# A memory-augmented transformer on one core: the recorded order of its tasks from the 1200th on replaced by another

## The chip, the cores and the metric

The kernel runs on one core of one Trainium2 chip. Its time is the device time of one execution in microseconds (us); the profile of that execution starts with the first instruction and ends with the last. The engines are PE (TensorE, the matmuls), PEld (the weight loads of PE, which overlap its matmuls), DVE (VectorE), ACT (ScalarE), POOL (GpSimd) and SP (SyncE). SP and POOL also issue the transfers (DMA): SP on the queue called hardware_dynamic, POOL on the one called software_dynamic.

## The reference

Two pairs of layers on x of 2048 x 512 in bf16: an attention with a recurrent memory, a gated feed-forward network, and both once more with the same weights.

```python
def _A_ref(x, mem0, Wq, Wk, Wv, Wo, seg_len):      # 32 heads of 128, 8 memory rows, segments of 32
    mem = mem0
    for s in range(n_seg):                          # 64 segments, one after another
        h = jnp.concatenate([mem, x[:, s * seg_len:(s + 1) * seg_len, :]], axis=1)
        q, k, v = (jnp.einsum('btd,dhe->bhte', h, W) for W in (Wq, Wk, Wv))
        scores = jnp.where(mask, jnp.einsum('bhqe,bhke->bhqk', q, k) * scale, -1000000000.0)
        o = jnp.einsum('bhqk,bhke->bhqe', _softmax(scores), v)
        o = jnp.einsum('bhte,hed->btd', o, Wo)
        mem = o[:, :M, :]                           # the memory of the next segment
        outs.append(o[:, M:, :])

def _B_ref(x, w_gate, w_up, w_down):                # 512 -> 1792 -> 512
    return jnp.einsum('bsf,fd->bsd', _sigmoid(x @ w_gate) * (x @ w_up), w_down)

x = x + _A_ref(_layernorm(x), ...)
x = x + _B_ref(_layernorm(x), ...)
x = x + _A_ref(_layernorm(x), ...)
x = x + _B_ref(_layernorm(x), ...)
```

(Shortened: the reference writes the three projections and the products out one by one.)

## The kernel before

**Steps.** The segments of one attention layer depend on each other through the memory, so the kernel goes through them in 70 steps (`emit_step(t)`). From step 6 on the second attention layer runs six segments behind the first, and one step does segment t of layer 1 and segment t - 6 of layer 2 together, with 2 x 40 = 80 columns. Four segments make a block; after each block a feed-forward pass (`ffn`) follows for its 128 rows, with the weights streamed again each time.

**One step.** PE makes q and k for three heads at a time (line 868, weights wq_sb and wk_sb stay in SBUF), ACT copies them out of the bank (qku), PE makes the scores (line 904), DVE and ACT do the softmax (lines 918 to 939), PE transposes the probabilities (line 950), ACT or DVE copies them (ptsb), PE multiplies them with the values (line 976), ACT copies that (otsb), and PE multiplies with wo_sb (line 995). The values are not where line 976 needs them: the part that depends on the memory is made in `strips` (line 762), copied to sst, and moved by transfers into vsb (`add_strips`); the part that depends on x alone is made ahead for a block (`v_pass`, line 635), copied to vst, written to the DRAM scratch scr, and read back into vsb. Line 976 waits for all of these transfers (the keys "vs" and "vx"). The feed-forward pass multiplies with wg and wu (line 1097) and wd (line 1120), which POOL loads in pieces of 256 KB (lines 1089, 1090 and 1114).

**What sets the order.** `trace` first adds 13,976 tasks to a `Planner`, each with the engines that may run it, a planned duration, and the keys that it reads and writes. A task on PE is a group of matmuls. `Planner.plan` doesn't search: it reads the order of all tasks, and one bit for each task that may run on either of two engines (copies: ACT or DVE; many transfers: SP or POOL), from SEQUENCE, a packed text in the file. The order gives each engine its own in-order program and also decides which buffers and banks a task gets.

**What the planner derives from the order.** `replay` goes through the tasks in the recorded order with a model of durations and transfer latencies (the constants LAT, BUS, LEAD, TAIL and others) and gives each task a planned start. Two things are made from these. For a weight load on POOL of 300,000 modelled bytes or more it picks a PE task (`pace`), and `run` makes the load wait for that task. And `warm` looks at the planned idle time of PE ahead of each PE task:

```python
            if gap > 250.0 and on:                              # line 346
                ...
                if cold or lo < 0.6 * self.SPAN:
                    n = int((gap - 120.0) * 2.4 - (min(tk.start, self.COLD) - end) * 1.2 * cold) // P
                    if n > 0:
                        fill[tk.idx] = (on[0], n)
```

Here `on` are the banks that the task takes, `lo` is the least planned PE work in a stretch of SPAN = 3413 ns around the gap, `cold` is true only near the start, and n counts groups of 128 columns. `run` then issues, ahead of such a task, matmuls of zeros (the tile hot) into that bank, of up to 512 columns each, on line 1214. They are called fillers below. `replay` and `warm` are the same code in both kernels.

Of the kernel before, what the change touches and what calls it, by code (L numbers as in the profile page):

```python
# [1293 lines left out]
```

## Time and profile before

| | us |
|---|---|
| median of 3 runs | 1747.95 |
| lowest and highest of them | 1744.44 and 1748.0 |
| span of the profiled execution | 1747.1 |
| PE busy | 1733.4 |
| DVE busy | 1248.4 |
| ACT busy | 1128.5 |
| POOL busy | 859.0 |

The span runs from the first to the last instruction of the execution that was profiled; no other time of that execution is shown. Lines such as "L868 PE MATMUL bank<-hT,wq_sb 128x80 x6656 | 485.9, 202 | 0.0" are groups: line of the kernel, engine, operation, output and inputs, shape, count, then busy time, mean duration of one in ns, and idle time of the engine before them. In a timeline the first number is the start, the second the length of the merged piece; the pieces overlap, since a matmul's record includes its way through the array, so that the distance between starts is what a matmul costs PE. A wait line names who waited, for what, the total, the number of times and the longest.

### The profile page before, as it was taken

The numbers are of one execution on the slowest core, as the hardware profiler recorded it, in microseconds if no ns is written. First come the engines' busy times: TensorE is split into PE (matmuls) and PEld (weight loads), VectorE is DVE, ScalarE is ACT, GpSimd is POOL, SyncE is SP. The second block draws the span as 40 slices with busy tenths as digits, with TensorE's granted clock in tenths as the row PEclk, the third lists the DMA queues.
The fourth block names the chain that finished last, engine by engine and source line by source line (L and its number), as shares of the span: only waits on it lengthen the run. The fifth ranks groups of instructions, "written<-read, shape, count | busy, mean of one in ns | idle before, by whom it ended". The sixth has DMA issues, their size and how long they took to land.

```text
span 1747.1 us, 91842 instructions
## 1 busy us (share of the span) xinstructions
PE 1733.4 (99%) x39162; PEld 1491.8 (85%) x39162; DVE 1248.4 (71%) x4208; ACT 1128.5 (65%) x3119; POOL 859.0 (49%) x1367
## 2 busy tenths in 40 slices
PE   9999999999999999999999999999999999999998
PEld 4688789889898988989888888989888888988886
DVE  5677777677767776786777767776777776767676
ACT  3576777566666766666666666666665666666564
POOL 5624345635544554445445554544455364454543
PEclk9999999999999999999999999999999999999999
DMA  8935355645645555545555464545455464554644
GB/s 285 320 100 155 109 151 161 195 113 153 174 130 163 156 159 143 165 125 164 152 148 158 136 184 128 166 138 153 132 174 166 139 174 128 144 156 131 178 120 134
DMA packets 145583, 273.41 MB, mean 156 GB/s; under 512 B 39686, under 2 KB 86018, under 8 KB 145174
## 3 DMA queue, kind: packets, MB, share of 16 engines
q0 software_dynamic: 72944, 198.79, 39.8%
q1 hardware_dynamic: 72230, 68.75, 13.3%
q8 instruction: 307, 5.03, 1.2%
q14 instruction: 102, 0.84, 0.2%
HBM read 221.78 MB, written 27.07 MB: 142 GB/s over the span
## 4 chain that ended last, share of the span: by engine, by line
PE 94%; DMA 3%; DVE 1%; SPq 1%; issue 1%; POOL 0%; ACT 0%; POOLq 0%; ACTq 0%
PE bank L868 34%; PE bank L995 17%; PE bank L1097 12%; PE bank L762 8%; PE bank L635 6%; PE bank L1120 6%; PE bank L904 4%; PE bank L976 4%; PE bank L950 2%; PE bank L595 1%; PE bank L1214 1%; DMA wk_sb<-in_A_Wk_dram 1%; DMA wo_sb<-in_A_Wo_dram 0%; PE bank L1065 0%; DMA scr<-wu 0%
## 5 line engine op out<-in xcount | busy, mean ns | idle before, releaser
L868 PE MATMUL bank<-hT,wq_sb 128*128 128x80 bf16 (+3 forms) x8960 | 616.4, 198 | 1.0 <-DVE hT L1008 0.3
L868 PE MATMUL bank<-hT,wk_sb 128*128 128x80 bf16 (+3 forms) x8960 | 616.3, 198 | 0.8 <-DMA wk_sb<-in_A_Wk_dram 0.6
L1228 ACT CAST qku<-bank 128x480 bf16<-128x480 f32 (+4 forms) x770 | 384.7, 508 | 223.7 <-PE bank L868 194.6
L868 PEld LDWEIGHTS <-wq_sb 128*128 128x128 bf16 x8960 | 454.2, 99 | 32.1 <-issue 15.1
L868 PEld LDWEIGHTS <-wk_sb 128*128 128x128 bf16 x8960 | 446.9, 99 | 1.1 <-DMA wk_sb<-in_A_Wk_dram 0.7
L995 PE MATMUL bank<-otsb,wo_sb 128*128 128x80 bf16 (+1 forms) x8960 | 360.2, 198 | 2.2 <-DMA wo_sb<-in_A_Wo_dram 1.3
L918 DVE TENSOR_TENSOR st<-bank,cst 40x240 f32<-40x240 f32 (+3 forms) x768 | 280.5, 368 | 113.2 <-PE bank L904 97.5
L995 PEld LDWEIGHTS <-wo_sb 128*128 128x128 bf16 x8960 | 336.6, 99 | 15.5 <-DMA wo_sb<-in_A_Wo_dram 2.0
L1228 ACT CAST otsb<-bank 128x480 bf16<-128x480 f32 (+3 forms) x420 | 200.2, 483 | 83.4 <-PE bank L976 52.8
L1090 POOL DMA_DIRECT2D wu<-in_B_w_up_dram x217 | 166.5, 768 | 170.0 <-PE bank L950 36.4
L1114 POOL DMA_DIRECT2D wd<-in_B_w_down_dram x217 | 156.9, 723 | 182.0 <-PE bank L1120 39.6
L1224 POOL DMA_DIRECT2D vsb<-sst x351 | 178.2, 512 | 129.6 <-ACT sst L1228 64.7
L1089 POOL DMA_DIRECT2D wg<-in_B_w_gate_dram x217 | 166.4, 767 | 138.1 <-PE bank L1097 56.7
L928 ACT ACTIVATE st<-st 80x240 f32<-80x240 f32 (+3 forms) x420 | 159.2, 381 | 58.0 <-DVE st L925 54.8
L1097 PE MATMUL bank<-xnT,wg 128*128 128x128 bf16 (+2 forms) x1784 | 171.5, 218 | 0.0
L1097 PE MATMUL bank<-xnT,wu 128*128 128x128 bf16 (+2 forms) x1784 | 171.1, 218 | 0.0
L930 DVE TENSOR_REDUCE small<-st 80x6 f32<-80x240 f32 (+3 forms) x420 | 151.5, 363 | 23.4 <-ACT st L928 20.2
L1220 ACT ACTIVATE ptsb<-bank,small 120x160 bf16<-120x160 bf16 (+3 forms) x430 | 156.6, 386 | 17.2 <-PE bank L950 10.7
L904 PE MATMUL bank<-qku 128*128 128x80 bf16 (+1 forms) x2240 | 162.7, 197 | 1.0 <-issue 0.9
L925 DVE TENSOR_TENSOR st<-st,small 80x240 f32<-80x240 f32 (+3 forms) x420 | 155.0, 370 | 5.7
L939 DVE TENSOR_TENSOR pb<-st,small 80x240 bf16<-80x240 f32 (+3 forms) x420 | 154.1, 370 | 5.7
L923 DVE TENSOR_REDUCE small<-st 80x6 f32<-80x240 f32 (+3 forms) x420 | 152.5, 364 | 6.2
(108 smaller groups left out, 2554.1 us busy)
## 6 DMA issues: line engine op xcount, KB each, us to landing
wg<-in_B_w_gate_dram POOLq DMA_DIRECT2D x220, 256.0 KB, 4.2
wu<-in_B_w_up_dram POOLq DMA_DIRECT2D x220, 256.0 KB, 4.2
wd<-in_B_w_down_dram POOLq DMA_DIRECT2D x220, 256.0 KB, 3.9
vsb<-scr SPq DMA_DIRECT2D x137, 66.0 KB
scr<-vst SPq DMA_DIRECT2D x90, 96.0 KB
vsb<-scr POOLq DMA_DIRECT2D x93, 66.0 KB, 3.4
vsb<-sst SPq DMA_DIRECT2D x179, 32.0 KB
vsb<-sst POOLq DMA_DIRECT2D x169, 32.0 KB, 2.8
```

The lines of the kernel that those rows point to most:

```text
L868: nc.tensor.matmul(o_ap, lhsT=W[:, c, h * P:(h + 1) * P], rhs=mv(c), start=(c == 0), stop=(c == DC - 1))
L904: nc.tensor.matmul(s_all(SB)[:, w0 + i, :], lhsT=fview(qku[:, i, 0, 0:1], [(1, P)]), rhs=qku[:, i, 1, 0:ncol], start=True, stop=True)
L918: pl.add("DVE", dve_ns(n, True), lambda gsz=gsz, hs=hs, st=st, SB=SB, pj_=pj_, npj_=npj_, mk=mk, idx=idx: nc.vector.tensor_tensor(out=st[p ...
L928: pl.add("ACT", act_ns(n), lambda hs=hs, st=st: nc.scalar.activation(out=st[pr, hs], in_=st[pr, hs], func=ACTF.Exp, scale=self.scale), r=s ...
L995: nc.tensor.matmul(WB[:, c * ncol:(c + 1) * ncol], lhsT=self.wo[:, h, c * P:(c + 1) * P], rhs=otsb[:, hl, 0:ncol], start=(h == 0 and c == ...
L1089: pl.add("POOL", 760, lambda wg=wg, fs=fs: nc.gpsimd.dma_start(out=wg[:], in_=self.wgv[:, :, fs]), r=[("wo", self.H - 1)], w=[gk] + bt, la ...
L1090: pl.add("POOL", 760, lambda wu=wu, fs=fs: nc.gpsimd.dma_start(out=wu[:], in_=self.wuv[:, :, fs]), r=[("wo", self.H - 1)], w=[uk] + bt, la ...
L1097: nc.tensor.matmul(gu[:, 2 * i + k, 0:n], lhsT=W[:, c, i * P:(i + 1) * P], rhs=xnT[:, c, rw], start=(c == 0), stop=(c == DC - 1))
L1114: pl.add("POOL", 760, lambda wd=wd, ip=ip: nc.gpsimd.dma_start(out=wd[:], in_=self.wdv[:, 2 * ip:2 * ip + 2, :]), w=[dk] + (["boot"] if se ...
L1220: nc.scalar.activation(out=dst, in_=src, func=ACTF.Copy, scale=by)
L1224: {"SP": nc.sync, "POOL": nc.gpsimd}[tk.on].dma_start(out=got[1], in_=got[2])
L1228: nc.scalar.copy(out=dst, in_=src)
```

## The change

SEQUENCE, and nothing else, is another text: 88 lines of packed text in place of 91. Unpacked, the first 1200 tasks stand in the same order as before; of the 13,976 tasks, 12,468 have another place. Some tasks that may run on either of two engines have changed engine: 275 transfers from SP to POOL and 245 from POOL to SP, 226 copies from DVE to ACT and 197 from ACT to DVE. The order comes from a search over many drawn transfer latencies; the search itself is not part of the file.

```diff
 SEQUENCE = r"""
-;BKuib6o%lfB&)8j78VFm3*TORJaEeTpTegcj@45cPG=tDu9Cop`gL7BsLuS#OcT}UGbOE%Rvw4_#4%#$D8H!O&97}fvKE=gc~;{D3dThKHFPlwO_o2ZQj%uAntT#b%`=yVSW>zYu00~2SQlskfdun`!ZJ6nE#G~2&?9uc>M
...
+;BKuiOkDs8fB&)8j78VFm3*TORJaEeTpTegcj@45cPG=tDu9Cop`gL7BsLuS#OcT}UGbOE%Rvw4_#4%#$D8H!O&97}fvKE=gc~;{D3dThKHFPlwO_o2ZQj%uAntT#b%`=yVSW>zYu00~2SQlskfdun`!ZJ6nE#G~2&?9uc>MLJNnK-
...
 """
```

The new text is three lines shorter, so each line behind it has a number three lower in the changed kernel: line 976 there is 973, line 1214 is 1211.

More of the change, by code (lines that the diff above doesn't have):

```diff
@@ new lines @@
+i1i0YD(h(Op*uWQ$hJP;Bf$yQikUbL75}K_CCXhEehY;YAKq*!3Uc%Xg9$$6Whfxhc_;!XnaeXsWETb0$)eOXEs9v^~2GKd~)jxtdFb@D02?xh_1fp?KW&fTj7T(bbip<45F%z<Q6F`V0&|>^`^b?PqJ8zT^ZMn>Wcly5FU_gC4bg<
+ct_t?VIQ91i<1%2up=CHX$olDJee`BwTFh$S(4b<7J|(ro=5g4z*Oc`7TsdGat-Gu458Br)V!dZ#th}Vr^2k08taR4-icZnRx1)Jh)>hE~oGsr}+TM9h@FLc<(r!wd_Q)l$@#>Gc$q3H~Iu8B@vGI?!$xWWOMXWIIV?oY_(Nj>~oPr
+OXhF>kb>ie>V?Z|=S{vC&%nc&mvj8fqJ`ng-1GxzLO~&l^?UGKdDeu&>V<rn<D;V-Yi3I0U}(d~*VL}SKef_{vihFam*0lE<Q@4Z?!Z?qE-e`<gdP%rljFd}%1N*?wM}ezvJGP{k@D$cH#i)?<HymwHhj3y7oDOxbMj(>d6(b!Q+d{
@@ new lines @@
+(|M_LSlswhN@?|yLvdUV@!>Nk$<yx}-KsEGBSCDfS=C0>x5r{0(p(QEni`j5ECChA3J3+en0nRK&Hcp0NU*(n0!X;LFq2XQO*by|ReBHqg1wB7#*M>TgpbMjBrkTU*99uz+Vk!4**({(MLwZLEUo#F;deCBV;>LUumfbyI^#!VVbWP
+5k$-hsK6I{?fV507ZWSJA|AKq%5F`{1CT0QO{)ll|TX=i|DlMvH>_RLPExPwr>G%@9qVJCKh;rJ^&U%*#K4T$Bg>MQlaj#5~$wQ1)H`pM<6emLUsv5wZa)l=){WY>u1(PrWo8E^2D1I#8XB}8^Ls58~C54o1mj9OA=J+4cPJ+C~sE6
+k-4%RqgqmQ@h`>lOlqIj>AJFkinT?O$TWwjR^@6_cLn`TAVN35#yQY<*I21kz9Ns_M+*Pe5gr82={@l%VCFW^OjXNT&v-JXZ0S8#SWWNRKWQPnYAKzHradadQn4f$;G}>_d4yW04N8b?H9Mw|2s5Xzb{n+^LkU5(ns%q)-{`@GLBrM
@@ new lines @@
+(tz$ql*20Y`Cw){%g;Fl%~s#-G~l0N}ay(ES$kOVS`jMVn3mC7pl}g1MPyOmL}dZtOkjDr~4V}U#Dpn^%oM-;HM|<`@aHzgS-QhaJQw<mppwr7q$_-+dF-cDH@qyx0A#!oeH7Hb?+f`q6Q%1{``g&R)-$>jCW-v9$A&$b=41@4|@+Z
+wI6&EA{+B?a}by4AbW1X_R^Gdv#$JPb_{I%Wp4g|=2o{MbxfLQ1EVhTZ$*P@@IaN>Guee><f99(hn>$qZ>EZ}J?7Q)^gWGEz6tEHHb+#sev=ywHcw$4#o?qGLKgd^blmB9JqWy(Gm}B<J~5gD&aw$ja^g^D1966B$EBF0Ix_6?z%6d
+>DXT1WAXz^Ce=l)9TWCv+p#mO8n!=>B*g*~zTp3A3IOnk^6EMg8!oFudP6CLS8DX=#v55*zlR*;TWqe(+6^2>Gbf5+RL+2K^@X%<<W<Rb^AEE#n)!omJLEK9eA1N5J4scl~t{f0tI}542fhFWkRx9w<_%@tpPq*#(dEwOa+FD+>=rQ
@@ new lines @@
+Kyp3QVU>(a6sXXCsd<5ACzr%qcxg4xX~AH)yeW~hgy-cOa^ruo$=Qx|JHnAf)AD~+hf#R`Ov7iprckPxmqA?pcC>u(~$kmZCm+3&?=1ZF`7Q@^qnwXaUp^2_JiVfzojWF@y3pTtvUExhlLYa2tyet#%32#sP#3%F~o$syju&a_ztN<
+7a-J|zMb*z|PML~OIHrHkcm>I^babF>g6SVE>-wMW#7)v`lyu6(7d@CSx_Y)U!pC4Bkq6V*|qd${a`=;hNfoznO@mAn7r*Np3LSZ^z9GA*>{$X6pyfCe)x=kcEhYO)(THL?L)K&RnS7`+xw-B4S!1C4Tf_!*rgD3l$@>lW7oq-<5u<
+uX<Autc6#II88tzO!48AqM@Gy5zbIuk8qEyE@AnS!+Rnc3`_*<ykqN8G#+A{(cDoTERx~necgroevdVZW+(=D+uJ4oQhLps(OufKoNvKUY9k4Od8}71Ma@5Q)=6q^9HWM>?bBLno;ZPV}guG0;Fxowm^4wW6TqB>87~7R%QBy>+mZA
@@ new lines @@
+1h=TJnM5xIp@oUk^O8C~DO6l}MUJZkc-gNl?Q1>?3VTPmy0WGkX|2l&RB1w$BoU27L1Kwz0Rfld?wT)u!)U^$HSNiJRGpV}fD<066ybGt3QoWB@?NuGZ?%6=ebiIM6vtgQ**C+wJz^?TO_lm)7S}pu#qhUzwCH7ipx;171LCmZ7CAS
+L6eAp`jn{VexkB@@4*3FCSVC$HK)}!YL8l@y<+wcID}R7=&8s~c^~Gju_-km!X<|xQ%!9`P-%ynFZ6RWJsjMkLh4*`z)~(=Qws&W<Qeu)mLd095w8vs(fJUThQyk3OitRpiEz2!430XaY5oG?L=>cuONS-Koh*3lhRZi}Q*3#U$$#p
+8vBlRguN|t+>7QZ#RVOVZXFA&sc>dW#iKxj|YZhP2rWY`)6egMR$-|yppGVdgiNZD|T?PK?}s+HhC1$Fi3d)jgAauLBr5Ex`N<$9p@DUV^wB7mR8`=s?KEUo2HS$oVIhf+lXY>1i8nvG*eR59&&8D4cTJ55ReNGd#+<+}J<n<`67TS
@@ new lines @@
+j(4So8aMVVZ6v(pk46-ECb;=g>JZPp77$AzmfU9rW3?LUE>eln}k1kz#X0uq8%i^BS}lI3FfDq{<h)t;n=x8(2gY7(a+ppPUHqNH{Ra07(%Gt^>F=PE}uC#x^9?J&9bx=Q%MtwXGCMH3U`$sPo0fcodHuaX#)UjC!UA*w9|Dk%|ODX
+M(L{-zX57qk6V2T<=1yy$T~~M3l(}*V8eG*MXVLFyK}ygTi$OVW$y`u0O{4rYGlHDQ&T~8ucxMPTXx*<GsBgSblBT(SA~Gd%H#{C3&%+O>jlv{4MBr_QZ!*{7Ze^&0Ad4UYKYZ=9C%n!BrMgp?OCQgg~VZ*@d0s+}hs*&Lp<3<zgq%
+N5)s6OwGh$ePKo*+irY7Uef5HePKwcN5dGae@feY9|uJ^DxZNyyyCxrNWlZOk2)To3Lw&BAdPn%&~@=NQXgHT-iCO+8wJBPA8u1lRI}n45wmYCO6a2-dDgh~HJ#GMr;;_TR+O0au|ft|R#HpY8mk|ini79{h5C4*=%{^V-II1XC-?b
@@ new lines @@
+TQ%Q0kjetxP_VBYBTz)212yoOkq&Dmf%&li)*~II=cm3O{c{C5?FxPOei&aO{5oflxPgy(NEs;nb6=FTR;=^+bJYE{2Z43lxGYr1~@*Xi<Bquf@SAu&l>-*y+o0Qv)Zu_bBVp^B&@=J3-BA+(!^V=ES(11+hb8=R(4}nTCEw^Po%0+
+O9kkU+uj*_NxA%X!-G@p`ivBI8o_U3{<=^I1kxdfsZQ6_@s4cQsQU52ZNd!UXPUWmR>ariy9cQ=K`<<4Y0j~wa6YbvKdcFoH2*v7L%o<giEev_-?vTGRB*b@&-5-g5{GHyu&hLQ=od8yX}m66QHgA)npif(7G+U$nj6Mx1RMN3zv7*
+AZtXdev*q!JI6`Hw)XA#CMph7EgW=sACZx1^Tgj$KR-wIdpWgYuFSvktGcsTGA-lEmT!{n_Cy9MJD_)AuzAdQeU^p>unNtZwgDXefcP1!!YRFv)hPwIaCS{o$h*jcqy2CnvWy4h|f5hT3~)(yY?btUgLRB4zKEktsa6E8+us@u~Q2M
@@ new lines @@
+{$Tm7RrqdDPj(Cc$Q!jMCkhqJ`?b_NA0xWUKT%Ok3D#Uk{AL2Dh;yKNS~P)njO*hZjW8DS)`+A1+uakkv%a`^}bkti<apW=Nu9XHj<$@TWe&?PGSKb@$ym#j#Th7wSmI8f+M4eGU|JEuzHxI&^H99b5AVe&z|io_5H|(QtAV!Xja8Z
+<c^*5VErwer(E6_t(P9jHE*b$-t&iTk`O(>u9dUYRue`TcL};rJS49#2{N{&l~9+QM_*pxaCFGg=A(h!Q9w|RfGOuOfC&GN=e1Q1p@B$6ztbmhzOZa)ZdpJJpLZz^iW-6r=1zL+y=$mfbSNEY(#`+NNm=hZk90aC<Q&6lY9F_uG540
+7ZL8GL-5I$1C%!b<85M&{+FHz<04oPj^&r6e1V18Y6EE=_VG==3@1pbSx-b5IA<?P&o~T$QD8Hag6MHh~FfC`w6UQf|7-1m=PVaVkNvf$7M;3v4myCSyk^s>mH37m-y(T3sPs;S+kj}5uncGk~Q%aajY^M8CIpoA1is_O!-kf%%L5+
@@ new lines @@
+#rg;*!!!hbsx1ri#OPvaf*&YpDr5{<gMdcV6Wcn*!K@zTbIAp+#bzOaFwDPvVzBL74Q*5!2wImoaFa<Dt<1$`?ap;5HNPndj8b9VGKqiQF(X#KpDMkYeuUvt)RXSWPyX(g73+V#8$4VE5<_?7rhI`!qGAhI&j-nJR?cVsd`v4sEz%P
+HfL$j8)xbcznAREh>j38={GrD$v=iA^K&(GP5yS6~YqK<Rc}^6$~Md)y>%^|Er;^|F(~$y2R!E;gQ97f0qEW_vV%f*9(cEeYj2;KNKmA9^%yCOyP%0%os6$M!n>^8G7%K|8#&+|IUt+RSP9rdW%VmR#7<Qu#^M9IiWreFw{?u9dx@A
+xbrFpW>O-2GLxl+TPNd(lBFZJB$Z;X+QN7@ym6_=^BK@%N<+SpB>MTERt%0??bb#5VsROAxX2F3$a+x#h!m&3XBAA+y=fDkiC%d1%EeW8APPcqaP9x8f9e0iDB#!gLjQohxI6p)87>UVhp&Trm^ZA$PB)`^|iJM6?<d9S{rQJBU2Cd
@@ new lines @@
+h>l(HV^>U^X+&@%i}Fp!#IfL{GPgBfKwOSXz}%WJOt8D)N9ucj#^-!ZEuw85b=+n#>KXiFGdL%-R`l1`hltP?N*KVp7<W=qWRxN)8R%C6bK$(o#&gg-zPN8DP4KoktfejPQLFx$<!^=Tq{It$ff{^DBLlsKmd|b@C<)*lxzBk5{Qw6
+SG2TmaXdK#uU^NHs4ifk><{gCoUgd}nsKDdb)A1ijv770w^g4h(*g7~E<Zc3g7mziA7-dbS@4E!Bka*C(K{ek9pc=vl0E(_rmv%;UDHWrHd^;^f8p^Z9w2ypsJ#XBEG|kC@t1l$UxS)??=c!_AWVPvnrwfQHS2;F6>GGGCOKM>1jB!
+w&KUGAX0R^ETe#3I>Ly2k8RwD(0|8Isczfn3KivphdCB<eT6eF%#@cW|aj!=u^yzdW$Fdwqo?>9p*4<ApuH$EOngb*LS@M%3?*vlyxK~(yAWGkTM%+&0LRYS#bf(gr2@Z{bd{4un!qO<BiA5cz-@T4+H7m4c`w%0Ww%xiGzv#wxX$Y
@@ new lines @@
+((fa{E6c6e-Z&oOTiqbgt9_v>(|=vS64fWo7SHNajT?5g9tvYD{HfFU)NUp@jiRwIgcwZ;trp)g;w1kZEkuhjCq`g$NM|dayJ+69@LIHe>s*OcsSNed-Ub@_x;IE8TmsdvijUc;m-*zB2sInlv*S&#nTUjUrVRT7<SbP^&-5ZGGL6C
+oDI;sz2AJbh?&I8_BgkNvQi-eh@ko@eR1E#L`c-(n{mVYITNp9H$B2hOUz!P12%=JE$;)v3()em=yDJ_wQ>0x#3Su6EtZv&7KG(4N#8F>b4Pq7Dm=x`f$e4U$ONd!x;T$zIA{#JFf?V{{c!%sx82WAsm%DHYg1YyM<yBH{_9Hs=%HO
+YD(cWFmcS;j<g(>{m4ZtT<=bj6e~=zkx~rEIKU;rS}&~ysYn8PeT-g<ubMA`<0iqyZv^ZEY*LuLncT%!P%>&oCs5Sx2Rh)ToWw0-AT22Q+{e>k$}8e$gR>5a^+?wXxv77FX?ovlI;^APlgPBd%xkDayqimkbbjwss0}d%kCpj%AohS
@@ new lines @@
++l9|`#yj~5kK6V~T+QlhX)2t(EPl6yssLgGXIkY0h_ry^*3s4!!;miFIgu%m0rTSfoBr@&Top_U2;s^AK%X6dD*~vW5K$@&~XOAGrZBis^$A`23iymxC5sQ%kzAStx0y)TM>3J-0L6*}{#!hswj0~OuU=8jK0G-fNUGd_xxd0mfPs!
+(%k$1Rx#X<a7f0{>PzRoX`JyTD6*#WOtT7cxtbLG3J?K^tFGS~|9ej&CzusOyA(tP1JKuz366Zu-?-a}d0wW9RkgJ;_k%h&lf(t{9n`?KSe6IM2?8i%Hni$jV~<|HWoB#_J5J!w@qMN$AX)`CcNWN<@SGyJ|qKQtd>26m3ofig16K2
+%rQZA8MleoL9#PUU0eohtX;2vFebQdTuZYqcYudfDLMa&o_216SV*jaPw1zL1FY2)y|N;=QfW?yW!?<J?g^)p>ci_f`A)XY>JbB?@QN4Om21ieE!dFI*Q6huaaQ_EDm7n2g~k7o~Jf`Rh&W&p@<qO<?>l^pUveNaQ+6dt+r15<2}`k
@@ new lines @@
+X1`S66BlDk&IC%J~j0c{txXk(ve<62)|8jk3XTOn@~D+3bJu*^Lh_@)H|e11a!MF{Kwf+Aqu&8*D_uI%tFh6hZk6Qe*1hs`k9595yMEIBs6MQ)Jz1HN4gGuQa_o$&1pnR1Z;gsya{q+>M3JwS?*H!sIFjfE_TjiH{uO~>N^ZxGw01g
+Mvz+?J!P#nw~~@n-s~KVO6L&9hSIlF_^|rW&^0n_4w!J5l|zA9x(OMCXs~PMq2K7?Rr3-mAJ7KcWSk*)Zu5$om}=$SROmx4JHel${nfg5t->3=R!UzBF`6OOMiw~snJTd*_z8uDUW^x-PmD>AT82pvd$cIO&0Rq=st}^y@*s4I5Wa0
+u>3Lpr94WIZEqH2*iRU{}fM^lYE@h7`saX=tQZeu^tlHa%Z178M!?(3XNgPb=`*FY@#$FxL$^R+2(bK1DB6=E8B)tI6!N%=!A_ln`Du3q791Ae(MiQpZKLI|oKPp1z^IK%i{l^cY?;Py-pZ47Qj#>qJ-qj+-<RjJV=K*&G5>7hZfhT
@@ new lines @@
+YeIDo7wgnA{0QS)pWHkF-P&(~^h3bCF|;w+RY8sFkuQze9vUC>2kyLiINr0rRwBmIL&Ji@(csBP0<4Wht@nYkPc*uL*M>w@DKDiu(C;42hX=l@y)-KQ`mlpQYiMvhHQH3#{i0emJjN7^-Xi>ju^tQwb4m(#>qg885@j0}yKPvnf5Fl
+1-SYO4VMJ+++dSl?N6i<lb!v%G?>yCL9@Ww{S~c|iy;CeZ=yA7y1zkyqonGQRRh^FSA(2uC!Kzd4_-QI&2;m}sSNk+vB_Y8r4Lp{WU`2H&-#@>=+g1t>UlqpY!7v8=ozIc?tB!h~j9aP4g&*>164&t@*U6OGh?liX|sFC1t_hqU?#{
+rOULM)t&4*Gt!TpLTE-Hq+UxpPCbD61v!hENy!D^9j&+8Fz<_3vgS$g~EU#iiAy}*;=xxks*(f>Lx=w|9|?rtaUA2XJ?W&ATkbC#{%3YDH|myj;t7{17`63d6)rR@GZLdKCn^|d{|!r$_^q|L`MMgorQ#zIZ|JDo@+!DQPZmMB)YA~
@@ new lines @@
+7GYR%WTwdR0-d$=WQ25}$mTEW&3l?;>+m)Nc&BknMcqKg0G)54kAfi-3E^-;qNxpnHE$*=vZK=hVibeCYWPb!$tbnR2&3o_hle5<ay}B;g>`hG{*fr0JiT#Mq=+HEA~bUe2)#VI>W)6NgngaEN#SDFMlq*s!vb2S?UJ6eBHCbtJc&x
+t%R1f5;lGTxTFMhiYju5%>1e(gfmwfoA-l}xEE&jyf!D}^Gt7@_TGz=OsBN0|R!Wh#xcnSZ+gxk|Ktr{9qB_j~)ZneBj^hWT5GgU5EG$C@HHMOUTcf&(Wfv=$^XvX1BGyGFUbU3>^S*mZE~6FkuIffFMSaY~&tuhANr*<c6Te#XF-f
+PARvkkS(3HKQMPzx+s~qrA2Ub(9pCmd+)T3hZznGh%hyu)4PS;eynb5-$mX`RsQ5c6r4_mp^&PjIl3KYI+Yj49s`PJ1X0Ff<yf#^e(R#(qz;|CD>#*Jkcvn%ByHWtpVm*9@<n8_kz#vo(qf1DP8XH*wH9mS7W$%X*ujWF0#dzhKgs2
@@ new lines @@
+O61g|`Lfgma)Fn&i7@8Bi0iw2<%43Y7fK=2Fo?l^UY?tGPsL|D}?L9DVp`n{wcYX~PS?$4UopPboQ%5Jj`5_wi#Ws~9f`|J2<PRhF;G61o+-X!W$CCUu3v!7OOU@OutODzcbAu5cluGZfVfxd);U`<kqOndTKVSy|Eo$QVpFXjSQWV
+EH6Tsy;_}Tm}EI-1HyU^f|KOJW$xH812eu_8ZR@*2q4^uzb7z!qxC|#pAws4_xAhgr1LF4^XhzPEDhx>}vsRn^@oi6~fS%T<Ztpo!6%87*>Cw0hbOq6tAWb*^p+cjt-p-cA}cdBi8nADw87W(A007gU*AA4Vd%M1BK_=+;3p&7{A!f
+0K{#V%!cUz=2PmbpYo=Trb|(aoJcT45|L2(A6X65HASF|q8;-%Dw%+0rGRE%K5f`X>;aweXjd^4Pn`MEIU3^JXZWgZu%~h4Q|XnsqN`8|O}w8Air&dhQk+rEnSrIdLD9COKFRkrYk)42Jdsid`;vk+4DWJpi4^j6Vo9pN+o4404YFZ
@@ L145 @@
+@*&O87B
 """
```

130 lines of the change are left out of this document (39 added, 91 removed).

## The prediction

> **What bounds the kernel now.** I read the page's totals first, then its chain of waits, then the stages, then the waits of PE alone, because the first two decide whether an order can still win anything.
>
> ```profile
> span 1747.1 us, 91842 instructions
> PE 1733.4 (99%) x39162; PEld 1491.8 (85%) x39162; DVE 1248.4 (71%) x4208; ACT 1128.5 (65%) x3119; POOL 859.0 (49%) x1367
> ...
> PE 94%; DMA 3%; DVE 1%; SPq 1%; issue 1%; POOL 0%; ACT 0%; POOLq 0%; ACTq 0%
> ```
>
> PE is busy for 99% of the span, and the chain that ended last is PE for 94% of it. Visible idle time of PE is 1747.1 - 1733.4 = 13.7 us. The span is the profiled execution's only time shown; it lies 0.85 us under the median of the three runs, 1747.95, and inside their 1744.44 to 1748.0. Sums below are made on the span, and 0.85 is added at the end.
>
> The stages (microseconds; busy time by engine, then granted clock, DMA share, GB/s) and the waits of PE:
>
> ```profile
> 0.00:100.00 100.00, 94.45 (x1449) 57.07 (x1450) 58.40 (x179) 49.29 (x145) 55.65 (x121) 1.00 0.85 278
> ...
> 400.00:600.00 200.00, 199.90 (x4427) 176.11 (x4425) 142.37 (x479) 131.46 (x347) 102.91 (x162) 1.00 0.54 154
> ...
> 1600.00:1747.00 147.00, 140.85 (x3909) 120.21 (x3901) 103.43 (x359) 85.73 (x278) 68.43 (x102) 1.00 0.50 143
> ```
> ```profile
> PE bank L635 <- DMA wv_sb<-in_A_Wv_dram: 2.4, 2, 1.9
> ...
> PE bank L976 <- DMA wg<-in_B_w_gate_dram: 0.2, 1, 0.2
> ```
>
> Of the 13.7 us, 5.6 stand in the first 100 us, which the change leaves alone, and 6.2 in the last 147. In the middle PE loses about 0.1 us in 200, its longest wait anywhere is 1.9 us, and line 976 (attention times values, which needs the transfers into vsb) waited once, for 0.2 us. An order that tolerates late transfers has nothing to recover there.
>
> A matmul's record lasts about 0.2 us although the next one starts after 0.036 us, so short waits hide inside busy time. I bound them by what the work takes at the steadiest start-to-start distances:
>
> ```profile
> 1397.30 0.31 PE L868 MATMUL bank<-hT,wq_sb 128*128 128x80 bf16 x4
> ...
> 1398.88 0.31 PE L868 MATMUL bank<-hT,wk_sb 128*128 128x80 bf16 x4
> 1399.12 1.91 PE L762 MATMUL bank<-wv_sb,hT 128*32 128x512 bf16 x32
> 1400.96 0.25 PE L904 MATMUL bank<-qku 128*128 128x80 bf16 x2
> ```
> ```profile
> 1559.77 1.68 PE L673 MATMUL bank<-wv_sb,xvl 128*64 128x512 bf16 x14
> 1561.38 0.25 PE L950 MATMUL bank<-cst,pb 80*128 80x80 bf16 x2
> ...
> 1562.10 0.71 PE L1214 MATMUL bank<-hot 128*128 128x512 bf16 x3
> 1562.64 0.38 PE L976 MATMUL bank<-ptsb,vsb 120*128 120x120 bf16 x4
> ```
> ```profile
> L868 PE MATMUL bank<-hT,wk_sb 128*128 128x80 bf16 x6656 | 485.9, 202 | 0.0
> L868 PE MATMUL bank<-hT,wq_sb 128*128 128x80 bf16 x6656 | 485.6, 202 | 0.3 <-DVE hT L1008 0.3
> L995 PE MATMUL bank<-otsb,wo_sb 128*128 128x80 bf16 x7424 | 311.5, 201 | 0.0
> ```
>
> The three fillers of line 1214 at 1562.10 hold 512 + 512 + 256 = 1280 columns, as the built program has them, and the next matmul starts 0.54 us later: 0.4219 ns per column, the lowest price in these rows. The program before has 4,709,504 columns. Of them 1,196,032 are line 762's (2,336 matmuls, 32 in 1.84 us, so 134.3 us) and 32,768 line 673's (64 matmuls, 14 in 1.61 us, so 7.4 us). The other 3,480,704 take at least 1,468.5 us at 0.4219. The 20,736 matmuls of 80 columns in lines 868 and 995 cost more than that: from 1397.30 to 1398.88 stand 11 groups of four, so 35.9 ns each against 33.75, and 45 us are added. Together 1,655 us are the least the work can take by these rows. Everything else in the span, waits seen and hidden and the dearer small matmuls, is at most 1747.1 - 1655 = 92 us. I put the small matmuls' part at 50, an estimate: the 3,072 of 40 columns in lines 868 and 995 start 25 ns apart, as the rows below show, 8.1 ns above 40 columns at 0.4219 (25 us in all), and some 11,700 others lie about 2.2 ns above theirs, as those of 80 do (25 us). That leaves about 40 us of waiting in the program, the visible 13.7 among it.
>
> ```profile
> 1717.05 0.25 PE L868 MATMUL bank<-hT,wk_sb 128*128 128x40 bf16 x4
> 1717.15 0.25 PE L868 MATMUL bank<-hT,wq_sb 128*128 128x40 bf16 x4
> ```
>
> **The change part by part.** Reading the two built programs engine by engine: the first 1200 of 13,976 tasks are in the same order and every computing line issues the same instructions, 39,104 matmuls outside line 1214 in both. But the program isn't only reordered.
>
> *Fillers.* Planner.warm puts zero matmuls on line 1214 ahead of a PE task where the plan of the recorded order shows PE idle for more than 250 ns and less than 60% busy around it. The before program has 58 of them in 16 bursts; the after program has 418 in 42 bursts. In units of 128 columns that is 207 before and 1,621 after: 1,414 units or 180,992 columns more, in 360 more matmuls. 24 of the added bursts (1,281 units) stand before line 976 in steps 10 to 68, the largest 128 units. They are instructions in PE's own queue and run whether or not the wait they were meant for occurs. By the 0.4219 ns above they take 180,992 x 0.4219 = 76.4 us. A second price: twelve 512-column matmuls of line 635 from 10.23 to 12.83, 216.7 ns each, or 0.4232 per column, give 76.6.
>
> ```profile
> 10.23 2.76 PE L635 MATMUL bank<-wv_sb,xvf 128*128 128x512 bf16 x12
> 12.83 0.61 PE L595 MATMUL bank<-cst,xn 128*128 128x128 bf16 x8
> ```
>
> I take 76.5. Where no wait is there to fill, all of it is added to the chain, since PE is that chain. It could be hidden only by waits that the new order brings, and then the waits are the added time instead; by existing waits at most for the 40 us above, which I count under the rivals.
>
> *What a burst leaves behind.* At 1562.10 line 976 followed at the filler price with no rest. At 204.71 five units should take 0.27 us and the next matmul started after 0.46:
>
> ```profile
> 204.71 0.43 PE L1214 MATMUL bank<-hot 128*128 128x512 bf16 x2
> 205.17 0.28 PE L904 MATMUL bank<-qku 128*128 128x80 bf16 x3
> ```
>
> So a burst leaves 0 to 0.19 us; for 26 added bursts 0 to 5 us. I take 1.5, nearer the first row, because it stands before line 976 as most of the new ones do.
>
> *Matmuls in another order.* 2,234 of the 4,202 PE tasks change place, by 20 places at most. The work is the same. A gain is at most the 40 us of waits. The loss I bound by the worst stage before the end, the first one that the change reaches:
>
> ```profile
> 200.00:400.00 200.00, 199.30 (x4582) 174.82 (x4579) 149.41 (x516) 138.81 (x396) 100.52 (x158) 1.00 0.55 153
> ```
>
> 0.7 us in 200, and 5.4 over the 1,550 from there on. I take 0, by the other middle stages, which lose 0.1 at the same DMA share.
>
> *Transfers and casts on other engines.* 275 transfers go from SP to POOL and 245 back, a net 30 more on POOL; a net 29 casts go from VectorE to ScalarE.
>
> ```profile
> L1224 POOL DMA_DIRECT2D vsb<-sst x351 | 178.2, 512 | 129.6 <-ACT sst L1228 64.7
> L1228 ACT CAST qku<-bank 128x480 bf16<-128x480 f32 (+4 forms) x770 | 384.7, 508 | 223.7 <-PE bank L868 194.6
> ```
>
> 30 x 0.51 = 15 us more on POOL (49% busy), 29 x 0.51 = 15 us more on ScalarE (65%). PE covers both; without that cover each is at most 15 us. Queued behind a moved transfer on POOL are weight loads of lines 1089, 1090 and 1114, and lines 1097 and 1120 wait for those. I take 0, and +15 as the upper end.
>
> Sum: 1747.1 + 76.5 + 1.5 + 0 + 0 = 1825.1, plus 0.85 for the median: 1826 us.
>
> **The rivals.**
>
> *The waits are real and longer than their fillers.* Transfers on SP stand in line behind others, and SP already waits long for its sources:
>
> ```profile
> SPq L1224 <- DVE sst L1230: 326.0, 33, 19.4
> ...
> vsb<-sst POOLq DMA_DIRECT2D x169, 32.0 KB, 2.8
> ```
>
> If half of the 24 bursts at line 976 leave a wait of one landing time, 2.8 us, the sum grows by 34 to 1860; if all do, by 67 to 1893. For it: SP can be held up to 19.4 us. Against: PE waited 0.2 us in all at line 976 for such things, and a filler of several us gives the transfer that much more time. [...]
>
> *The fillers take the place of waits.* Part of the 40 us disappears, because other engines and queues catch up during the bursts. Losing the whole would give 1786, losing 25 gives 1801, losing the 8.1 us of visible idle behind the first 100 us 1818. Against it: the visible waits between 100 and 1600 are 13.7 - 5.6 - 6.2 = 1.9 us in all, and nearly all new bursts are in that part.
>
> *Not slower.* The bursts fall into waits that are there already and as long as they: in the 24 places before line 976, PE would already stand 76.5 us. From 76.5 us of such waits on, the time is 1748. For it stands only the bound of 92 us, if the small shapes cost nothing over their columns; against it the rows of 40 columns above and the single wait of 0.2 us at that line. Fillers that ran for nothing would do the same, and the burst at 1562.10 had its full price.
>
> *The change does what it says and nothing else*, an order alone: then 1748, within some us. The added matmuls in the built program exclude it; it is part of the last case.
>
> **How the numbers follow.** Forecast 1826 with its own range 1818 to 1836: 70%. Real waits behind the fillers: 15%. Fillers in the place of waits: 13%. Not slower: 2%, half within 0.2% (3.5 us, about what a measurement of this kernel can tell from no change) and half below. Slower is therefore 98%. The range runs from 1808 (18 us of waits gone) to 1852 (9 waits of 2.8 us left, or the 15 us on POOL and some of them): outside lie about half of each middle rival and the last case, some 16%.
>
> **What would show it.** In the changed profile line 1214 (three lines up in that file, so 1211) has 418 matmuls, and their busy time rises by about 76.5 us, most of it in steps 10 to 68 between 250 and 1750 us. PE stays at 99%, the clock at 1.00, and the waits of PE at line 976 stay below some us. If those waits reach 20 us, the first rival holds; if the span grows by less than the fillers' time, the second. I am wrong if the fillers' start-to-start distance differs from 0.42 ns per column, or if the span differs from before by more or less than they take.

## The result and the profile after

| | before | after |
|---|---|---|
| median of 5 runs, us | 1747.4 | 1824.55 |
| lowest to highest | 1743.06 to 1748.0 | 1823.24 to 1825.37 |
| ratio, 95% interval | | 1.0444 (1.043 to 1.0457) |
| span of the profiled execution | 1747.1 | 1821.5 |

The changed kernel is slower by 4.4%, which on 1747.4 is 77.6 us, between 75.1 and 79.8 by the interval. Line numbers of the changed kernel are three lower than those of the kernel before. The two spans differ by 74.4 us only: in every run with both figures on record the time is 1.65 to 2.11 us above the span, so the profiled execution of before took some 1749 us, more than its median, and the one of the changed kernel was the fastest of its five.

From the page of the changed kernel, the totals and the chain that answer to those shown of before:

```profile
span 1821.5 us, 92519 instructions
PE 1808.1 (99%) x39522; PEld 1526.3 (84%) x39522; DVE 1253.4 (69%) x4179; ACT 1145.2 (63%) x3148; POOL 869.7 (48%) x1397
...
PE 92%; DMA 4%; issue 1%; SPq 1%; POOL 1%; DVE 1%; ACT 0%; POOLq 0%
```

PE has 360 matmuls more and is busy for 74.7 us more, as against 74.4 us more of span. Its visible idle time is 1821.5 - 1808.1 = 13.4 us, where it was 13.7. So the time did not go into waits. The groups by line say where it went: among the matmuls only the fillers grew by more than 0.2 us. Line 1094, for one, stayed as it was. The kernel before comes first:

```profile
L1214 PE MATMUL bank<-hot 128*128 128x512 bf16 (+3 forms) x58 | 16.5, 410 | 1.1 <-DVE cst L484 1.1
L1097 PE MATMUL bank<-xnT,wg 128*128 128x128 bf16 (+2 forms) x1784 | 171.5, 218 | 0.0
```
```profile
L1211 PE MATMUL bank<-hot 128*128 128x512 bf16 (+2 forms) x418 | 96.7, 379 | 1.1 <-DVE cst L481 1.1
L1094 PE MATMUL bank<-xnT,wg 128*128 128x128 bf16 (+2 forms) x1784 | 171.4, 218 | 0.2 <-DMA wg<-in_B_w_gate_dram 0.2
```

The fillers' records cover 96.7 us; in the kernel before they covered 16.5 (58 of them). The 80.2 us between the two hold 26 more ends of a burst, and a burst's record runs on past its last start. One burst of 37 units (4,736 columns) shows by how much:

```profile
1503.28 2.16 PE L1211 MATMUL bank<-hot 128*128 128x512 bf16 x10
1505.28 0.58 PE L973 MATMUL bank<-ptsb,vsb 120*128 120x120 bf16 x8
```

The next matmul starts 2.00 us after the burst began (0.4223 ns per column), so 0.16 us of each record lies under the next line's work. (In the trace of before, a matmul of 8 columns on line 568 has a record of 164 ns on average and one of 512 on line 635 one of 379: some 0.16 us over their columns at 0.4219, in both.) 80.2 - 26 x 0.16 = 76.0 us is what PE spends on the added bursts. By stage (busy time of the fillers on PE and PEld, granted clock, DMA share, GB/s), the middle of the kernel before first, then the whole of the changed one:

```profile
400.00:1400.00 1000.00, 0.00 (x0) 0.00 (x0) 1.00 0.54 152
```
```profile
0.00:200.00 200.00, 14.74 (x54) 5.31 (x54) 1.00 0.66 206
200.00:1600.00 1400.00, 74.28 (x332) 31.30 (x332) 1.00 0.50 144
1600.00:1821.00 221.00, 7.67 (x32) 2.76 (x32) 1.00 0.47 139
```

The middle of the program, where the kernel before had no filler, is spaced out by them. The waits of PE at line 973 (attention times values, 976 before), ahead of which most bursts stand, are one line:

```profile
PE bank L973 <- DVE ptsb L1219: 0.2, 1, 0.2
```

### The profile page after: what moved, and what is told of

It is laid out like the page before. It is cut to its first block, busy times and chain, and to the rows that moved or that the text cites. A ratio compares the mean times of both kernels' runs of the same rounds, so it can differ in the third digit from the quotient of the medians.

```text
span 1821.5 us, 92519 instructions
## 1 busy us (share of the span) xinstructions
PE 1808.1 (99%) x39522; PEld 1526.3 (84%) x39522; DVE 1253.4 (69%) x4179; ACT 1145.2 (63%) x3148; POOL 869.7 (48%) x1397
## 4 chain that ended last, share of the span: by engine, by line
PE 92%; DMA 4%; issue 1%; SPq 1%; POOL 1%; DVE 1%; ACT 0%; POOLq 0%
PE bank L865 32%; PE bank L992 16%; PE bank L1094 11%; PE bank L759 7%; PE bank L632 6%; PE bank L1117 5%; PE bank L1211 4%; PE bank L901 4%; PE bank L973 4%; PE bank L947 2%; DMA wv_sb<-in_A_Wv_dram 1%; PE bank L592 1%; DMA wk_sb<-in_A_Wk_dram 1%; DMA wo_sb<-in_A_Wo_dram 0%; DMA wq_sb<-in_A_Wq_dram 0%
## 5 line engine op out<-in xcount | busy, mean ns | idle before, releaser
L1225 ACT CAST qku<-bank 128x480 bf16<-128x480 f32 (+3 forms) x770 | 383.3, 506 | 203.9 <-PE bank L865 177.7
L1087 POOL DMA_DIRECT2D wu<-in_B_w_up_dram x217 | 166.2, 766 | 142.4 <-PE bank L1094 40.8
L1217 ACT ACTIVATE ptsb<-bank,small 80x160 bf16<-80x160 bf16 (+4 forms) x443 | 162.7, 385 | 17.7 <-PE bank L947 11.2
L901 PE MATMUL bank<-qku 128*128 128x80 bf16 (+1 forms) x2240 | 158.2, 197 | 0.0
```

Of the source, the lines that this page charges most:

```text
L901: nc.tensor.matmul(s_all(SB)[:, w0 + i, :], lhsT=fview(qku[:, i, 0, 0:1], [(1, P)]), rhs=qku[:, i, 1, 0:ncol], start=True, stop=True)
L1087: pl.add("POOL", 760, lambda wu=wu, fs=fs: nc.gpsimd.dma_start(out=wu[:], in_=self.wuv[:, :, fs]), r=[("wo", self.H - 1)], w=[uk] + bt, la ...
L1217: nc.scalar.activation(out=dst, in_=src, func=ACTF.Copy, scale=by)
L1225: nc.scalar.copy(out=dst, in_=src)
```

## The experiments

Theory A: the planner's waits don't happen on the chip, so the bursts are pure cost and the order itself changes nothing. Rival B: the new order has the waits, and the bursts only stand in them. If B holds, taking the bursts away saves nothing.

### Take the bursts away, in both orders

```diff
             fill = self.pl.warm(order)
+            early = {tk.idx for tk in order[:1200]}
+            fill = {i: f for i, f in fill.items() if i in early}
```

> The changed order, without the fillers (line 1214's zero matmuls) at and behind the 1200th task: 1,494 units of 128 columns less. Theory A, the fillers stand where PE has no wait and are pure cost: 1824.6 - 1494 x 128 x 0.4219 ns (80.7 us) = 1744 us, between 1739 and 1752, and PE's visible waits at the line of attention times values stay under 3 us. Rival B, the planned waits are real and the fillers only stand in them: 1810 to 1825, with some 70 us of PE waits that become visible. Rival C, half and half (the fillers gave late transfers time that they need): 1775 to 1795.

> The order of before, without its 80 units of fillers at and behind the 1200th task. Theory A, pure cost there too: 1747.4 - 80 x 128 x 0.4219 ns (4.3 us) = 1743 us, and the difference to the changed order without fillers is what the order alone is worth, which A puts within 5 us either way. Rival B, these bursts stand in real waits: 1747, unchanged.

Measured beside a before of 1750.95 (21 runs): the changed order without late bursts takes 1750.79 us, ratio 1.0003 (0.9992 to 1.0013); the old order without its 80 units takes 1747.7, ratio 0.9989 (0.9981 to 0.9998). B is out: 4.41 points of 4.44 go with the bursts. The waits at line 973 in the changed order without them:

```profile
PE bank L973 <- DMA vsb<-scr: 0.5, 1, 0.5
PE bank L973 <- ACT ptsb L1227: 0.4, 1, 0.4
PE bank L973 <- DVE ptsb L1221: 0.2, 1, 0.2
PE bank L973 <- DMA vsb<-sst: 0.2, 1, 0.2
```

At that line 1.3 us in all come into view, where 24 bursts of together 1,281 units (69 us) had been put. On the ratio, 1.0444 - 1.0003 is 77.1 us for 1,494 units; at 0.4219 ns per column they would be 80.7, so 96% of the price was paid. In the old order 80 units (4.3 us by columns) gave back 0.11%, 1.9 us, with an interval from 0.3 to 3.3, less than their price: there the bursts seem to stand partly in real waits. The old order without late bursts has the lowest ratio of the study, by that tenth of a per cent; the two orders without late bursts differ by 0.14%, with intervals that just overlap.

### Half of each burst

```diff
+            early = {tk.idx for tk in order[:1200]}
+            fill = {i: (B, n if i in early else n // 2) for i, (B, n) in fill.items()}
```

> The changed order with each late burst cut to half its units, rounded down: 754 units fewer. Theory A, linear: 1824.6 - 754 x 128 x 0.4219 ns (40.7 us) = 1784 us, between 1779 and 1790. Rival B, waits behind the bursts take the freed time: 1815 to 1825. Rival C, waits appear only once the bursts are short: 1795 to 1812.

1787.97 us, ratio 1.0218 (1.0204 to 1.0232). Against the whole bursts 2.26 points are gone, 39.5 us. The rounding leaves 739 of the 1,494 late units, so 755 are gone (the expectation says 754), which cost 40.8 by columns: linear, as A has it. The absolute time lies towards the top of A's band because all runs of this chip, before's too (1750.95), were some 3.5 us longer.

### The same bursts in the old order

```diff
+            fill = {i: f for i, f in fill.items() if i in early}
+            extra = {1423: 7, 1075: 13, 1438: 56, 2390: 98, 11188: 128, 13711: 3}
...
+            fill.update({tk.idx: ([bf for bf in tk.acq if bf.pool.psum][0], extra[tk.idx]) for tk in order if tk.idx in extra})
```

(Six of the 36 entries are shown.)

> The order of before with the late bursts of the changed kernel, ahead of the same tasks and of the same length (1,494 units in place of 80). Theory A, the bursts cost the same in any order: 1747.4 + 1414 x 128 x 0.4219 ns (76.4 us) = 1824 us, between 1818 and 1830. Rival B, the added time belongs to the new order: 1747 to 1765, since the old order has no waits for them to cover and should be able to run... the fillers beside other work. Rival C, bursts at places that this order did not plan for push other work late as well: 1835 or more.

1824.53 us, ratio 1.0431 (1.0417 to 1.0446). The old order with the changed kernel's bursts is as slow as the changed kernel. Against the old order without late bursts that is 4.42 points, 77.2 us of the 80.7 that 1,494 units cost by columns. The new order isn't needed for the loss, so B falls; nor did the bursts cost more than their columns, so C falls too.

### Where the planned waits come from

In `replay` a transfer is planned to arrive no earlier than a cursor, `bus`, that all transfers push on in the order of the list. If a weight load with a late planned start stands ahead of a small transfer with an early one, the small one is planned behind it. One term less in the arrival:

```diff
-                tk.done = max(bus + self.TAIL, end + tk.lat + tk.slow * min(max(wbus - t, 0.0), self.BACK))
+                tk.done = max(0.0, end + tk.lat + tk.slow * min(max(wbus - t, 0.0), self.BACK))
```

With it the changed order gets 60 late units instead of 1,494, and the old order the same 80 as before; the early units fall from 127 to 93 in both. The model's own length of the program shows the same: with the term it gives 1729.5 us for the old order and 1817.6 for the changed one, without it 1725.6 and 1728.9.

> The changed order; in replay a transfer's planned arrival no longer takes the shared bus cursor into account (only its own latency), so warm makes 60 late units in place of 1,494 and 44 of 672 weight loads wait for another PE task, at most 5 PE tasks away. Theory A, the planned waits come from that cursor, which is pushed on in the order of the list and not of time, and no transfer is really late: equal to the changed order without late fillers (ratio 1.0003 there) plus at most 60 x 54 ns = 3 us: ratio 0.999 to 1.004. Rival, the cursor describes a real queue, and a plan without it sends the weight loads at bad times: ratio above 1.01, with PE waits at the feed-forward lines.

1748.75 us, ratio 0.9995 (0.9983 to 1.0007). The plan without the shared cursor is enough to lose no time, and the 44 weight loads that now wait for another PE task do no harm that can be measured. That the cursor made the planned waits follows from the plan alone, by the units and the lengths above. The run shows that PE loses nothing on the chip when the plan leaves the cursor out; it does not show how the transfers queue.

### Are late transfers tolerated better?

This is what the order was searched for, so both orders (without late bursts) got 629 more copies of 256 KB that nothing waits for: first issued by ScalarE, then by SP.

```diff
+        self.load = [dr.tile([P, DC * 2 * P], BF16, name=f"load{i}") for i in range(16)]
...
-            for tk in order:
+            for at, tk in enumerate(order):
+                if at >= 1400 and at % 20 == 0:
+                    k = at // 20
+                    nc.scalar.dma_start(out=self.load[k % 16][:, :].rearrange("p (c f) -> p c f", c=self.DC), in_=self.wgv[:, :, k % 7 * 2 * P:(k % 7 + 1) * 2 * P])
```

> The order of before without late fillers, and with 629 more copies of 256 KB (a piece of w_gate to a DRAM scratch that nobody reads), issued by ScalarE at every 20th place from the 1400th on. The transfer engines' share rises from 0.54 towards 0.85, and other transfers land later. Theory A, neither order has a margin that differs: both slow down alike, 1755 to 1850, and the difference to the next run is under 1%. Rival, the changed order tolerates lateness better, as a search over drawn latencies would make it: this run is slower than the next by over 1%.

> The changed order without late fillers and with the same 629 copies at the same places of the list. Theory A: within 1% of the run with the order of before. Rival: faster by over 1%. A third case, slower by over 1%, would mean that the changed order is the more sensitive one.

Old order 1839.71 us, ratio 1.0496 (1.0471 to 1.0521); changed order 1844.62, ratio 1.0531 (1.0504 to 1.0558). The intervals overlap, and the changed order is not the faster one. But PE's longest total there was not for a transfer; from the run with the old order:

```profile
PE bank L905 <- ACT qku L1234: 30.0, 30, 2.8
...
PE bank L977 <- DMA vsb<-scr: 3.1, 3, 1.7
```

ScalarE issues the copies and comes late with qku (0.8 us of such waits without the copies), so this pair says little of late transfers. With SP as the issuer (nc.sync in place of nc.scalar):

> As the run with extra traffic on the order of before, with the 629 copies issued by SP instead of ScalarE, since ScalarE's own time was a part of the loss there. Theory A: 1750 to 1850, less than with ScalarE, and within 1% of the next run. Rival: the changed order is faster by over 1% when the lateness comes from transfers alone.

> The changed order without late fillers and with the 629 copies issued by SP. Theory A: within 1% of the run with the order of before. Rival: faster than it by over 1%.

Old order 1855.32 us, ratio 1.0605 (1.0586 to 1.0624); changed order 1921.51, ratio 1.0982 (1.0945 to 1.1018). Two expectations missed: the old order was to lose less than with ScalarE as the issuer and lost more, and the two were to lie within 1%. What came is the third case of the run before: the changed order is 3.6% slower than the old one. The longest waits of PE at attention times values, old order first (line 977 there, 974 in the other):

```profile
PE bank L977 <- DMA vsb<-scr: 13.1, 5, 7.1
PE bank L977 <- DMA vsb<-sst: 12.7, 10, 4.3
...
PE bank L977 <- DMA wg<-in_B_w_gate_dram: 8.6, 2, 5.2
...
PE bank L977 <- DMA wd<-in_B_w_down_dram: 5.9, 2, 3.8
```
```profile
PE bank L974 <- DMA vsb<-sst: 53.5, 21, 8.6
PE bank L974 <- DMA vsb<-scr: 19.8, 8, 6.8
PE bank L974 <- issue: 13.4, 9, 6.9
PE bank L974 <- DMA wd<-in_B_w_down_dram: 7.6, 3, 3.9
```

With the shorter ones they are 51 us against 100. The mean granted clock fell as well, to 0.987 in the old order and 0.970 in the changed one: PE ran at 0.50 for 48 us in the one run and for 116 in the other, at waits such as the last section shows. Of the 67.5 us between the two spans 41.6 are idle time of PE, and 25.9 are the same matmuls taking longer. So the transfers into vsb come late more often in the changed order under this load, while without it the two orders are alike. One placement of the copies was run, at every 20th place of each list. Whether the changed order leaves these transfers less time, or the copies happen to stand worse in it, was not separated.

### The bursts under late transfers

The changed kernel with its bursts and with SP's copies, to see whether the planned waits and the real ones stand at the same places.

> The changed kernel with all its fillers and with the 629 copies issued by SP. Without the late fillers this was 1921.5 (ratio 1.0982). Theory A, a filler costs its columns only where PE has no wait; here PE waits at the line of attention times values for some 95 us, partly where the planned waits and so the bursts are, and after a long wait the clock falls to half: the bursts cost clearly less than their 77 us, 1925 to 1970, with fewer visible waits at that line and a granted clock nearer 1.00. Rival, the bursts stand elsewhere than the real waits: 1921.5 + 77 = 1998, between 1985 and 2010.

1931.0 us, ratio 1.1052 (1.1019 to 1.1086), so the bursts cost 0.70 points here, 12 us (4 to 21 by the intervals), in place of 77. The visible waits at line 974 are halved:

```profile
PE bank L974 <- DMA vsb<-sst: 31.4, 21, 3.9
...
PE bank L974 <- DMA vsb<-scr: 7.3, 6, 2.5
PE bank L974 <- issue: 5.0, 6, 3.5
...
PE bank L974 <- DMA wu<-in_B_w_up_dram: 2.0, 1, 2.0
```

With the shorter ones 100 us became 50, and the mean granted clock rose from 0.970 to 0.988. The places can be compared by counting PE's matmuls, fillers left out: of the 100 us without bursts, 57 stand within two matmuls of a place where the changed kernel has a burst. So the planner's marks meet somewhat more than half of this order's real waits under the load; in the kernel as it runs there are next to none to meet (1.3 us, as above).

### No filler at all

```diff
-            fill = self.pl.warm(order)
+            fill = {}
```

> The order of before without any filler: beside the 80 late units also the 127 of the first 1200 tasks, 91 + 7 + 11 of them in the first 10 us. Theory A, a filler only ever costs: 1747 - 2 (the late ones, as measured) - at most 1 us for the three bursts of 6 units in steps 1 to 3; the first bursts stand in a wait for the first transfer, so taking them out saves nothing: ratio 0.997 to 1.000. Rival, the first bursts bring PE to its full clock: without them the first matmuls run at a lower rate and the run is 1 to 5 us longer: ratio 1.000 to 1.003, with a granted clock under 1.00 or longer distances in the first 20 us.

1749.21 us, ratio 1.0002 (0.9992 to 1.0013), against 0.9989 for the old order that kept its early bursts. The intervals overlap, so a gain of some 2 us from the early bursts is likely but not settled. The sign that the rival named, longer distances in the first 20 us, is there:

```profile
7.92 0.61 PE L595 MATMUL bank<-cst,xn 128*128 128x128 bf16 x4 [7.92 <-DVE xn L586]
...
10.27 4.65 PE L635 MATMUL bank<-wv_sb,xvf 128*128 128x512 bf16 x12 [0.57 <-ACT xvf L1228]
14.76 0.61 PE L595 MATMUL bank<-cst,xn 128*128 128x128 bf16 x8
```

The twelve matmuls of line 635 take 4.49 us to the next line's start, where the prediction's rows have 2.60, and line 595 follows 1.93 us later (14.76 in place of 12.83).

## Why the prediction was right

*What bounds the kernel.* PE, in both kernels, with the same visible idle time (13.7 and 13.4 us). That an order has nothing to recover there held: the orders alone differ by 0.14%, and no version won more than about a tenth of a per cent. The 40 us of hidden waits were a bound that no run used up, and their size stays untested.

*Fillers.* The step that carried the forecast: 1,414 units at 0.4219 ns per column, 76.5 us. On PE the added bursts hold 76.0 us by the records; taken away from the new order, all 1,494 late units give back 77.1 of 80.7 us. The mechanism is shown from both sides, by taking the bursts from the new order and by putting them into the old. One remark in the sum is wrong, without effect on it: 0.4219 is not the lowest price per column in its rows, since line 762's matmuls of 512 columns start 57.5 ns apart; but the sum prices lines 762 and 673 by themselves.

*What a burst leaves behind.* With 1.5 us on top the change was to cost 78.0; it cost 77.6, between 75.1 and 79.8, which tells 1.5 from 0 as little as from a small gain. Three other pairs of runs (late bursts taken away, halved, put into the old order) give 96%, 97% and 96% of the columns' price. They lean towards a small gain, bursts that stand partly in a wait, but the 3.5 and 3.6 us of the two whole sets are hardly larger than the intervals, about 3 us each. The traces point the same way: behind 200 us, PE's waits for a named engine or transfer are 1.2 us in the changed kernel and 4.0 without its late bursts, 0.8 in the old order with these bursts and 4.3 without. (Waits that the profile can put down to nothing are left out, since three of these four traces lack some 216 matmul records.) So the term's sign was probably wrong, and this stays open. That the sum came within half a microsecond is partly luck: by the ratios the added bursts are 4.41 - 0.11 = 4.30 points, 75 us instead of 78, and the order by itself is the other 0.14, 2.4 us instead of 0, each with an uncertainty of about its distance from the forecast.

*Matmuls in another order; transfers and casts on other engines.* Both taken at 0. The ratio 1.0003 (0.9992 to 1.0013) of the changed order without late bursts is all of it together; POOL's busy time rose by 10.7 us and ScalarE's by 16.7, under PE.

*The rivals.* Real waits behind the bursts: not there, 0.2 us at line 973. Fillers in the place of waits: at most those 4%. Not slower, and an order alone: excluded by the time; as an order alone the change would have been no change. The weakness of the first rival was its condition, not its mechanism: with late transfers, its waits are there, more than half of them at the places of the bursts, and in all half as long with the bursts as without.

*The clock.* No stage showed a clock under 1.00 in the profiles before and after, so it was worth nothing here. Under extra traffic it did fall to 0.50, at a wait of 8.63 us and at one of 1.71 among others, as told below.

## What to carry to other kernels

Where a plan feeds back into the program (fillers, anchors for loads), a new order is not only an order: count the built program's instructions line by line before you think about latencies. A filler is a bet that a planned wait is real, and on an engine that is the bound it costs nearly its whole length (96% here) when the wait isn't there; take the waits from a trace, not from the plan. And test what a change was searched for by itself: under the one lateness tried here that reached the transfers, the order that was drawn for late transfers was the more sensitive one.

## What the runs showed of the hardware

In the changed order with SP's copies the granted clock fell to 0.50 at waits of PE and was 1.00 again later. First the timeline around a wait of 8.63 us, then the stages (the columns as before; the clock is the third number from the end):

```profile
307.33 0.46 PE L974 MATMUL bank<-ptsb,vsb 120*128 120x120 bf16 x3 [8.63 <-DMA vsb<-sst]
...
307.65 1.80 PE L993 MATMUL bank<-otsb,wo_sb 128*128 128x80 bf16 x24
309.25 0.33 PE L974 MATMUL bank<-ptsb,vsb 80*128 80x80 bf16 x2
```
```profile
290.00:298.00 8.00, 8.00 (x189) 7.53 (x186) 7.58 (x29) 7.59 (x28) 4.78 (x8) 1.00 0.85 243
298.00:307.00 9.00, 0.69 (x19) 0.54 (x16) 0.26 (x2) 0.61 (x2) 2.72 (x5) 0.77 1.06 353
307.00:310.00 3.00, 2.67 (x40) 2.70 (x41) 0.35 (x2) 0.88 (x3) 0.00 (x0) 0.50 0.11 32
310.00:314.00 4.00, 4.00 (x69) 4.00 (x67) 0.78 (x3) 0.52 (x2) 0.35 (x1) 0.61 0.31 82
314.00:320.00 6.00, 6.00 (x170) 4.88 (x167) 4.35 (x12) 4.31 (x12) 3.44 (x7) 1.00 0.43 124
```

From 298 to 307, nearly all of it the wait, the clock is 0.77 on average. In the 3 us behind it, it is 0.50, and the 24 matmuls of 80 columns take 1.60 us from start to start, where the 24 at 296.04, in the stage at 1.00, took 0.85. From 314 on it is 1.00. In the trace's own records of the clock the fall is at 302.89 and the rise at 313.13, some 4 us into the wait and 5.8 us after work resumed. That is 10.24 us at 0.50. The 24 falls in this trace last 3.41, 6.83 or 10.24 us (15, 8 and 1 of them), 116 us in all; the mean of 0.970 over 1920.0 us gives 115.

Another of them stands behind a wait of only 1.71 us, which ended at 1851.63. PE had been busy for 1.70 of the 3.41 us up to 1852.54; the clock was 0.50 in the 3.41 us from there, and 1.00 behind them:

```profile
1849.13:1852.54 3.41, 1.70 (x53) 1.11 (x42) 1.19 (x5) 1.33 (x3) 1.52 (x3) 1.00 0.52 151
1852.54:1855.95 3.41, 3.41 (x91) 3.41 (x88) 3.10 (x10) 1.72 (x5) 0.00 (x0) 0.50 0.80 227
1855.95:1858.00 2.05, 2.05 (x50) 1.81 (x47) 1.39 (x5) 1.31 (x5) 1.20 (x2) 1.00 0.95 280
```

From how long a wait on the clock falls, these rows don't show.

At the very start the granted clock isn't a guide: in the old order without any filler it is given as 1.00 for the stage from 10 to 20 us, in which line 635's first matmuls started 374 ns apart on average (4.49 us for 12) instead of 217, and four transposes of 128 columns at 7.92 took 0.61 us where the four at 8.67 in the kernel before took 0.39. The clock's records in that trace begin with a rise to full at 14.12 us, and in the two profiled kernels at 6.54 (before) and 5.77 (after); what lies ahead of the first record is given as 1.00.

```profile
10.00:20.00 10.00, 9.73 (x43) 4.30 (x44) 5.72 (x16) 3.62 (x7) 4.96 (x12) 1.00 0.89 283
```
